# A planner that counts a load as a transfer plus a latency, shorter scale chains, and a new table of ranks

## The chip, the cores and the metric

The kernel runs on one core of a Trainium2 chip. Its engines work side by side: TensorE (PE in the rows) multiplies matrices, VectorE (DVE) and ScalarE (ACT) work elementwise, GpSimd (POOL) does some elementwise work too, and SyncE (SP) issues the DMAs that bring inputs from the device's memory. Each engine takes its own instructions strictly in the order in which they were written, and waits at an instruction until what it needs is there. The metric is the device time of one execution in microseconds (us); three runs and one profiled execution of the kernel before are at hand.

## The reference

Attention with four batches, eight heads, 576 positions and 64 values per head; half the heads see a local band of 32, the other half positions with the same remainder modulo 32. Its output, 2304 tokens of 512 values, goes through two feed-forward blocks.

```python
scores = scale * np.matmul(q, k.transpose(0, 1, 3, 2))
scores = np.where(masks[None, :, :, :], scores, -1000000000.0)
attn = softmax(scores)                       # with a small guard in the sum
x = (attn @ v) as 2304 x 512
h = x @ w_in;   x = np.maximum(0.01 * h, h) @ w_out                       # first block, 2048 wide
h = x @ w_in2;  out = (np.maximum(h, 0.0) + np.log1p(np.exp(-np.abs(h)))) @ w_out2
```

The weights arrive as 64-bit floats, two 32-bit words each.

## The kernel before, in words

**Products.** A float32 product is made of three float16 products: each operand is cut into a high part and the rest (`mm3`, L538 to L541). So a step of a projection is twelve matmuls of 288 columns (four slices of the sum by three), and nearly all of TensorE's time goes into these. Tokens of the first block are worked in eight units of 288 (units 0 and 1 belong to batch 0, 2 and 3 to batch 1, and so on), those of the second in nine of 256.

**Weights.** A quarter of a weight (2 MB) is loaded into one of four areas, `pair` in the rows (`Weight.load`, L156). VectorE finds its largest value (`largest`, L165), TensorE spreads it over the partitions (`to_all`, L131, written `pm`), VectorE works out a power of two (`scale`, about ten instructions on one number per partition, among them a reciprocal and a product, L196 and L197), and then VectorE and ScalarE turn the 64-bit words into a float16 pair: `low` (L171), `copy_sign` (L209) or `sink` (L219), `merge` (L230), `high` (L238), `rest` (L245, L253). The area is then free for the next load. Of the first block's input weight (W1) each quarter has its own scale; the output weights (O1, O2) have one scale over four quarters, so all four quarters of O2 are first loaded once for their largest value alone (`plan_largest`, `O2l`): load, `largest`, load, `largest`, one after another through one area.

**Attention.** For each batch, six pieces: `dots` (L362) on TensorE, the largest of each row on VectorE (`top`, L382, L390), the exponential on ScalarE, sums, a division spread on GpSimd (L464), a transposition on TensorE (`turn`, L473), a copy on ScalarE (`fetch`, L484), the product with v (`pv`, L496), and a cut in high and rest (L524, L531, L535). `factor` works out the batch's scale (L136 to L318).

**What sets the order.** All this is not run by a schedule on the chip: `Plan` is told every step with its engine, a cost in us, what it depends on and a rank name, and `Plan.run` plays the whole through in time, beginning at each engine with the step of lowest rank among those that could start about now. In that order the instructions are written. While TensorE has nothing in this play before 130 us, filler products of 512 columns are written (`idle`, L100). `RANKS` holds for each name a start and a slope. A step on SP is a load: its cost is how long SP's place in the play is taken, and whatever depends on it is counted ready `LOAD` later. The names: `W1r`, `W1m`, `O1r`, `O1m`, `W2`, `O2`, `O2l` are weight steps, `A0` to `A3` and `B0` to `B3` the early and late steps of attention, `G0` to `G3` the first projections of units 0 to 3, `S0` to `S3` the second ones, `M` both of the later units, `X`, `F`, `Fa`, `Fp`, `Fd`, `S`, `E` the second block.

Of the kernel before, what the change touches and what calls it, by code (L numbers as in the profile page):

```python
# [12 lines left out]
I32 = mybir.dt.int32  # L13
# [10 lines left out]
KC = DM // P  # L24
# [10 lines left out]
TINY = 2.0 ** -120  # L35
# [20 lines left out]
SIGNED = ("i1",)  # L56
# [6 lines left out]
def build(tc, qt, kl, ks, v, wi1, wo1, wi2, wo2, mloc, mstr, out):  # L63
    nc = tc.nc
    with ExitStack() as ctx:
# [84 lines left out]
        class Weight:  # L150
# [24 lines left out]
            def scale(self, q, g):  # L175
# [60 lines left out]
            def high(self, q, hl, by=None):  # L236
                by = (1.0 if self.name in SIGNED else SHARE) if by is None else by
                nc.scalar.activation(flat(hl[0]), self.f[q], AF.Copy, scale=by)  # L238
                self.hl[q] = hl

            def rest(self, q):
                hi, lo = self.hl[q]
                if self.name in SIGNED:
# [19 lines left out]
        class Attn:  # L263
# [47 lines left out]
            def factor(self):  # L311
# [3 lines left out]
                inv(self.ax, self.p2, 2.0 ** 14)  # L315
# [25 lines left out]
            def dots(self, half):  # L341
# [3 lines left out]
                ps = two_banks("ps", "sc" if self.b else "mm")  # L345
# [197 lines left out]
        def project(ps, wi, x, f):  # L543
            q, o = divmod(f, 4)
            sl = slice(o * P, (o + 1) * P)
            for c in range(KC):
                mm3(ps, wi.hl[q][0][:, c, sl], wi.hl[q][1][:, c, sl], x[0][:, c, :], x[1][:, c, :], c == 0, c == KC - 1)

        def gate1(x, f, g):
# [4 lines left out]
            def part(i):  # L554
                project(ps[:, i], W1, x, f + i)
# [24 lines left out]
        class Plan:  # L580


            HOP, SLACK, LOAD = 0.2, 0.5, 0.9
# [123 lines left out]
        def plan_loads(A, buf, where, after={}):  # L707
# [3 lines left out]
            for k, n in enumerate((0, 1, "v", 2, 3)):  # L711
                if n == "v":
                    ld[n] = plan.add("SP", 4.05, lambda: A.load_v(buf()), after.get("v", ()), (f"L{b}", k))
# [3 lines left out]
                    "SP", 1.65, lambda n=n, places=places: A.load_qk(n, *(w and w() for w in places)),  # L717
# [7 lines left out]
        def plan_attention(A, ld, after=(), behind=(), scaled=()):  # L725
# [17 lines left out]
            for half in range(6):  # L743
# [4 lines left out]
                    "PE", 2 * n * w / 975 + 0.12 * n * (A.mode[half] != "e"), A.dots, mine + [dots] * (half > 0), half,  # L748
                    take=["sc" if b else "mm"], free=mine * (half % 3 == 2), behind=behind,
# [49 lines left out]
        def plan_together(W, name, after, parts, then, w1):  # L799
# [6 lines left out]
            for q in range(4):  # L806
                ld = plan.add("SP", 5.9, lambda q=q: W.load(q, area(q)), after[q], ("L" + name, q))
# [29 lines left out]
        def plan_quarter(W, name, q, place, after, parts, after_read, then=None):  # L837
# [17 lines left out]
            ld = plan.add("SP", 5.9, lambda: W.load(q, area(place)), after, ("L" + name, q))  # L855
            x = step("DVE", 2.2, big, [ld], 0)
            y = step("PE", 0.1, over, [x], 0, take=["pt"])
            sc = step("DVE", 1.45 if then else 1.05, scale, [y], 0.3, free=[y])
            y = step("DVE", 1.14, lambda: W.low(q), [ld], 0.1, port=True)
            if W.name in SIGNED:  # L860
# [7 lines left out]
            if W.name in SIGNED and REST[q] == "Pool":  # L868
# [3 lines left out]
        def plan_largest(W, name, busy):  # L872
# [3 lines left out]
            for q in range(4):  # L876
                ld = plan.add("SP", 5.9, lambda q=q: W.load(q, area(1)), busy[1], ("L" + name, q))
# [22 lines left out]
        def plan_first(u, after, w, place, rank):  # L900
            b, half = divmod(u, 2)
            out = []
            for f in range(0, NF, 2):
                st = {}

                def products(i, f=f, st=st):
                    if f + i == 0:
                        gs[u] = place()
                    if i == 0:
                        st["then"] = gate1(xpart(at[b], half), f, gs[u])  # L910
                    st["then"][0](i)
# [5 lines left out]
                mm = step("PE", 1.473, lambda p=products: p(0), after + [w[f // 4]], take=["mm"])  # L917
                more = step("PE", 1.473, lambda p=products: p(1), [mm])
                bend = step("ACT", 0.65, then(1), [more], take=["t"], free=[mm])
                high = step("ACT", 0.58, then(2), [bend])  # L920
                rest = step("Pool", 1.25, then(3), [high], free=[bend])
                out += [(mm, high, rest), (more, high, rest)]
# [210 lines left out]
        for q in range(4):  # L1133
            step = lambda eng, cost, fn, deps, k, **kw: plan.add(eng, cost, fn, deps, ("O2", q + k), port=eng == "DVE")
            ld = plan.add("SP", 5.9, lambda q=q: O2.load(q, area(1)), busy[1], ("LO2", 4 + q))
# [319 lines left out]
```

## Time and profile before

| | us |
|---|---|
| median of three runs | 848.12 (845.75 to 849.96) |
| the profiled execution | 852.07 |
| its span, first to last instruction | 850.3 |
| TensorE busy | 827.4 (97% of the span) |
| ScalarE busy | 524.7 (62%) |
| VectorE busy | 488.1 (57%) |
| GpSimd busy | 255.6 (30%) |
| mean granted TensorE clock | 0.994 of full |

TensorE's busy time holds the filler products too, so a busy TensorE early on is not always a working one. The page cuts the span in 40 slices of 21 us: TensorE is at nine tenths or more in all but the first, the thirteenth (250 to 276 us, which shows 7) and the last; VectorE is at eight or nine tenths only up to about 105 us.

```
PE   8999999999997999999999999999999999999997
DVE  5998949634434525764003668776665756465453
DMA  9833320303455204420002200000000000000000
```

### The profile page before, as it was taken

What the parts mean: (1) busy time and instruction counts of PE and PEld (TensorE: products, weight loads), DVE (VectorE), ACT (ScalarE), POOL (GpSimd) and SP (SyncE); (2) the same over time, 40 slices, a digit from 0 to 9 for tenths busy, and PEclk for the clock granted to TensorE, in tenths of its full rate; (3) what the DMA queues carried; (4) which work ended last, traced back from release to release, by engine and by line L of the source; (5) the groups of instructions that cost most, each with busy time, mean ns of one, the idle gap of its engine ahead of it and who ended that gap; (6) DMA issues with size and microseconds to landing.
All of it is one profiled execution on the core that took longest, in us unless ns stands there. A gap on an engine that the chain in (4) does not pass through costs nothing.

```text
span 850.3 us, 17550 instructions
## 1 busy us (share of the span) xinstructions
PE 827.4 (97%) x7311; PEld 680.9 (80%) x7311; DVE 488.1 (57%) x1160; ACT 524.7 (62%) x961; POOL 255.6 (30%) x193
## 2 busy tenths in 40 slices
PE   8999999999997999999999999999999999999997
PEld 4567777777776777777777788888888888888886
DVE  5998949634434525764003668776665756465453
ACT  2799687457754334423416288878676777677671
POOL 2267776123342032001305032232313222222220
PEclk9999999999998999999999999999999999999999
DMA  9833320303455204420002200000000000000000
GB/s 367 371 128 122 136 99 2 133 4 114 153 202 198 100 1 141 158 86 15 2 1 100 99 2 2 25 2 26 2 25 2 25 2 27 1 26 25 3 26 25
DMA packets 10991, 63.27 MB, mean 74 GB/s; under 512 B 1344, under 2 KB 1440, under 8 KB 7840
## 3 DMA queue, kind: packets, MB, share of 16 engines
q1 hardware_dynamic: 10656, 62.00, 19.5%
q8 instruction: 57, 0.93, 0.5%
q14 instruction: 22, 0.18, 0.1%
q10 hardware_dynamic: 256, 0.16, 0.1%
HBM read 57.44 MB, written 4.72 MB: 73 GB/s over the span
## 4 chain that ended last, share of the span: by engine, by line
PE 80%; DVE 9%; DMA 7%; ACT 2%; issue 1%; SPq 1%; POOL 0%; DVEq 0%; ACTq 0%
PE h L539 13%; PE h L541 12%; PE h L540 12%; PE o L541 12%; PE o L539 12%; PE o L540 12%; DMA pair<-wo_dram 4%; PE ps L362 2%; DVE m L165 2%; PE po L496 2%; PE pt L473 1%; DVE s L390 1%; DVE pair L230 1%; DMA pair<-wi_dram 1%; DVE pair L219 1%
## 5 line engine op out<-in xcount | busy, mean ns | idle before, releaser
L539 PE MATMUL h<-x,w 128*128 128x256 f16 (+1 forms) x1088 | 303.7, 279 | 1.7 <-ACT t L560 1.7
L541 PE MATMUL h<-x,w 128*128 128x256 f16 (+1 forms) x1088 | 303.7, 279 | 0.0
L540 PE MATMUL h<-x,w 128*128 128x256 f16 (+1 forms) x1088 | 303.6, 279 | 0.0
L1255 POOL TENSOR_TENSOR pair<-pair,t 128x512 f32<-128x512 f32 x72 | 96.2, 1338 | 268.8 <-ACT t L1251 116.2
L566 POOL TENSOR_TENSOR g<-t,g 128x576 f16<-128x576 f32 x64 | 96.5, 1513 | 214.8 <-ACT g L563 214.8
L539 PE MATMUL o<-g,pair 128*128 128x288 f16 x512 | 147.6, 288 | 0.0
L541 PE MATMUL o<-g,pair 128*128 128x288 f16 x512 | 147.5, 288 | 0.1
L540 PE MATMUL o<-g,pair 128*128 128x288 f16 x512 | 147.5, 288 | 0.0
L1271 DVE SCALAR_TENSOR_TENSOR gr<-pair,x2b,gr 128x896 f16<-128x896 f32 x72 | 85.7, 1195 | 72.6 <-ACT gr L1267 71.4
L540 PEld LDWEIGHTS <-w 128*128 128x128 f16 x1088 | 106.3, 98 | 20.8 <-issue 2.1
L539 PEld LDWEIGHTS <-w 128*128 128x128 f16 x1088 | 106.3, 98 | 19.7
L541 PEld LDWEIGHTS <-w 128*128 128x128 f16 x1088 | 106.3, 98 | 19.7 <-POOL w L245 0.3
L1263 DVE TENSOR_TENSOR pair<-pair 128x128 f32<-128x128 f32 x288 | 75.6, 305 | 45.9 <-POOL pair L1255 43.3
L1267 ACT ACTIVATE gr<-pair,x2b 128x896 f16<-128x896 f32 x72 | 74.2, 1035 | 37.3 <-DVE pair L1263 28.5
L560 ACT ACTIVATE t<-h,gs 128x576 f32<-128x576 f32 x64 | 47.1, 736 | 55.2 <-PE h L541 50.4
L464 POOL TENSOR_TENSOR s<-s,sm 96x512 f32<-96x512 f32 (+3 forms) x48 | 50.5, 1070 | 93.0 <-DVE sm L459 50.0
L1238 ACT ACTIVATE t<-h,x2s 128x512 f32<-128x512 f32 x72 | 49.0, 680 | 43.1 <-PE h L541 42.9
L539 PE MATMUL o<-w,gr 128*128 128x256 f16 x270 | 73.6, 273 | 0.0
L540 PE MATMUL o<-w,gr 128*128 128x256 f16 x270 | 73.6, 273 | 0.0
L541 PE MATMUL o<-w,gr 128*128 128x256 f16 x270 | 73.6, 273 | 0.0
L541 PEld LDWEIGHTS <-pair 128*128 128x128 f16 x512 | 50.3, 98 | 13.4 <-DVE pair L253 0.4
L539 PEld LDWEIGHTS <-pair 128*128 128x128 f16 x512 | 50.4, 98 | 13.1
(136 smaller groups left out, 1350.3 us busy)
## 6 DMA issues: line engine op xcount, KB each, us to landing
pair<-wo_dram SPq DMA_DIRECT2D x12, 2048.0 KB, 8.0
pair<-wi_dram SPq DMA_DIRECT2D x8, 2048.0 KB, 10.0
out_dram<-pair SPq DMA_DIRECT2D x18, 256.0 KB, 2.1
q<-qt_dram SPq DMA_DIRECT2D x12, 288.0 KB, 4.6
v<-v_dram SPq DMA_DIRECT2D x2, 1408.0 KB, 15.1
pair<-v_dram SPq DMA_DIRECT2D x2, 1408.0 KB, 6.4
k<-ks_dram SPq DMA_DIRECT2D x7, 288.0 KB, 6.2
k<-kl_dram SPq DMA_DIRECT2D x5, 304.0 KB, 4.4
```

The lines of the kernel that those rows point to most:

```text
L165: nc.vector.tensor_reduce(out=m, in_=hi.bitcast(F32), axis=AX.XY, op=ALU.max, apply_absolute_value=True)
L464: nc.gpsimd.tensor_tensor(out=sv, in0=sv, in1=rs, op=ALU.mult)
L539: nc.tensor.matmul(ps, ah, bh, start=first, stop=False)
L540: nc.tensor.matmul(ps, ah, bl, start=False, stop=False)
L541: nc.tensor.matmul(ps, al, bh, start=False, stop=last)
L560: nc.scalar.activation(t, ps, AF.Prelu, scale=gates[f // 4], alpha=0.01)
L566: nc.gpsimd.tensor_tensor(out=g[:, 1, f : f + 2, :], in0=t, in1=g[:, 0, f : f + 2, :], op=ALU.subtract)
L1238: nc.scalar.activation(t, self.ps[k], AF.Prelu, scale=self.sc[:, k // 2 : k // 2 + 1], alpha=-1.0)
L1255: nc.gpsimd.tensor_tensor(out=r, in0=r, in1=self.a[k], op=ALU.add)
L1263: nc.vector.tensor_tensor(out=r[:, o], in0=r[:, x], in1=r[:, y], op=op)
L1267: nc.scalar.activation(self.a[k][:, 0], self.r[k][:, 1:], AF.Copy, scale=self.ag)
L1271: nc.vector.scalar_tensor_tensor(out=a[:, 1], in0=self.r[k][:, 1:], scalar=self.ag, in1=a[:, 0], op0=ALU.mult, op1=ALU.subtract)
```

## The change

Four things, of which the last follows from the others:

- `LOAD` goes from 0.9 to 2.6, and the costs of the loads on SP go down: a weight quarter from 5.9 to 5.15, v from 4.05 to 3.4, a pair of q and k from 1.65 to 1.5. Some other costs change by up to 0.2.
- A power of two is inverted by one integer instruction on its bits instead of a reciprocal and a product. This is done in `inv` (attention's `factor`, the second block's `factor` and `scales`) and in `Weight.scale` for W1's four quarters. The other weights keep the two instructions.
- `SIGNED` names quarters instead of a weight (all four of W1, as before); `EARLY` is empty, so the code that asks for it does what it did. `TINY` goes from 2^-120 to 2^-100.
- All numbers of `RANKS` are new (39 names).

```diff
-TINY = 2.0 ** -120
+TINY = 2.0 ** -100
...
-    "O1r": (-2072.090, 3.859), ... "W2": (870.356, 188.158), "X": (881.188, 1.772),
+    "O1r": (-3595.719, 0.065), ... "W2": (-3968.496, 59.142), "X": (854.645, 2.549),
...
-SIGNED = ("i1",)
+SIGNED = (("i1", 0), ("i1", 1), ("i1", 2), ("i1", 3))
+EARLY = ()
...
-        def inv(a, p2, mul):
-            nc.vector.reciprocal(out=a, in_=p2)
-            nc.vector.tensor_scalar(out=a, in0=a, scalar1=mul, scalar2=None, op0=ALU.mult)
+        def inv(a, p2, power):
+
+            nc.vector.tensor_scalar(
+                out=a.bitcast(I32), in0=p2.bitcast(I32), scalar1=-1.0, scalar2=(254.0 + power) * 2 ** 23,
+                op0=ALU.mult, op1=ALU.add,
+            )
...
-                nc.vector.reciprocal(out=s, in_=t)
-                nc.vector.tensor_scalar(
-                    out=s, in0=s, scalar1=2.0 ** -110 if self.name in SIGNED else 2.0 ** -98 / SINK, scalar2=None, op0=ALU.mult
-                )
+                if (self.name, q) in SIGNED:
+                    inv(s, t, -110)
+                else:
+                    nc.vector.reciprocal(out=s, in_=t)
+                    nc.vector.tensor_scalar(out=s, in0=s, scalar1=2.0 ** -98 / SINK, scalar2=None, op0=ALU.mult)
...
-            HOP, SLACK, LOAD = 0.2, 0.5, 0.9
+            HOP, SLACK, LOAD = 0.2, 0.5, 2.6
...
-                clock = collections.defaultdict(float, SP=1.7, PE=5.7)
+                clock = collections.defaultdict(float, SP=1.4, PE=5.7)
...
-                ld = plan.add("SP", 5.9, lambda q=q: W.load(q, area(1)), busy[1], ("L" + name, q))
+                ld = plan.add("SP", 5.15, lambda q=q: W.load(q, area(1)), busy[1], ("L" + name, q))
```

The order moves on every engine; the numbers of products, loads and attention steps stay. Filler products number 84 instead of 72, all of them still ahead of the first projection. Three places follow; the changed file's lines lie a few further down.

**GpSimd, batch 3's attention.** L464 (L469) spreads a piece of batch 3, L566 (L571) is the rest of a first projection, one for every two steps of TensorE. Before:

```order
L464 TENSOR_TENSOR s<-s,sm 96x512 x6
L464 TENSOR_TENSOR s<-s,sm 126x504
L566 TENSOR_TENSOR g<-t,g 128x576
L464 TENSOR_TENSOR s<-s,sm 126x504
L566 TENSOR_TENSOR g<-t,g 128x576 x7
L464 TENSOR_TENSOR s<-s,sm 108x432 x2
L464 TENSOR_TENSOR s<-s,sm 108x216 x2
L566 TENSOR_TENSOR g<-t,g 128x576 x24
```

Now:

```order
L469 TENSOR_TENSOR s<-s,sm 96x512 x6
L571 TENSOR_TENSOR g<-t,g 128x576 x16
L469 TENSOR_TENSOR s<-s,sm 126x504 x2
L469 TENSOR_TENSOR s<-s,sm 108x432 x2
L469 TENSOR_TENSOR s<-s,sm 108x216 x2
L571 TENSOR_TENSOR g<-t,g 128x576 x16
```

Between batch 3's third and fourth piece stand the first projections of two units (32 steps of TensorE) where that of one stood (16 steps).

**VectorE, the loads of O2 for its largest value.** L165 (L169) is `largest`, m_2947 (m_3211) the four values of O2, L531 (L536) the rest of a piece of batch 3, L1184 (L1198) a step of the second block. Before (a first `largest` of the four stands 17 rows higher, ahead of batch 3's tops):

```order
L1184 TENSOR_REDUCE m<-x_2137 128x1
L454 TENSOR_SCALAR sm<-sm,ix_2273,gx_2274 126x8
L459 RECIPROCAL sm<-sm 126x8
L165 TENSOR_REDUCE m_2947<-pair_128 128x1 x3
L935 TENSOR_SCALAR xs<-p2x_843,k_o_1711 128x1
L531 SCALAR_TENSOR_TENSOR x<-po,ax_2266,x 128x2x192
L390 ISA s,mx<-ps,ms 108x108
```

Now:

```order
L464 RECIPROCAL sm<-sm 96x8
L1198 TENSOR_REDUCE m<-x_2085 128x1
L169 TENSOR_REDUCE m_3211<-pair_128 128x1 x4
L889 TENSOR_REDUCE m<-m_3211 128x1
L169 TENSOR_REDUCE m<-pair_128 128x1
L949 TENSOR_SCALAR xs<-p2x_594,k_o_1659 128x1
L175 TENSOR_SCALAR pair_128<-pair_128 128x2048
L137 TENSOR_REDUCE g<-pm 128x1
```

The four `largest` of O2 stood around batch 3's tops and rests; now they stand together, with W2's first quarter (the second L169) behind them, ahead of every step of batch 3's fourth piece. On TensorE the `pm` that the last row waits for stands 32 first-projection steps, one `dots`, one `pv`, one `turn` and one second-projection step after batch 2's last `pv`, three second-projection steps and two turns.

**VectorE, up to the end of batch 0's attention.** L535 (L540) over 18x6 is batch 0's last rest, on which the first projection waits together with W1's first quarter (L245, L250). Before:

```order
L535 TENSOR_TENSOR x<-po,x 128x18x6 x2
L450 TENSOR_SCALAR sm<-sm 96x8
L459 RECIPROCAL sm<-sm 96x8
L171 TENSOR_SCALAR pair_128<-pair_128 128x2048
L209 TENSOR_SCALAR pair_128<-pair_128 128x2048
L450 TENSOR_SCALAR sm<-sm 96x8
```

Now:

```order
L137 TENSOR_REDUCE g<-pm 128x1
L141 TENSOR_SCALAR g<-g 128x1
L124 TENSOR_SCALAR p2x_594<-g 128x1
L146 TENSOR_SCALAR ax_595<-p2x_594 128x1
L322 TENSOR_SCALAR ix_601<-p2x_594 128x1
L323 TENSOR_SCALAR gx_602<-ix_601 128x1
L175 TENSOR_SCALAR pair_128<-pair_128 128x2048
L455 TENSOR_SCALAR sm<-sm 96x8
L464 RECIPROCAL sm<-sm 96x8
L214 TENSOR_SCALAR pair_128<-pair_128 128x2048
L395 ISA s,mx<-ps,ml 96x128
```

`low` and `copy_sign` of W1's second quarter (L171 and L209, now L175 and L214), batch 1's `factor` (L137 to L323) and the guard of batch 1's first piece stood behind batch 0's last rest; now they stand ahead of it, by one group of tops and the rest itself. `factor` has one instruction (L146) where L144 and L145 stood.

## Rows read from the trace of the kernel before

**Rows 1.** Busy time by stretch: engine busy us (instructions), TensorE clock, DMA share, GB/s

```profile
50.00:60.00 10.00, 9.61 (x83) 7.57 (x83) 9.93 (x8) 8.55 (x15) 8.18 (x4) 1.00 0.50 206
60.00:70.00 10.00, 7.75 (x83) 6.01 (x81) 9.83 (x44) 9.50 (x30) 8.76 (x5) 1.00 0.27 84
80.00:90.00 10.00, 8.68 (x81) 6.66 (x78) 7.70 (x29) 8.33 (x24) 10.00 (x7) 1.00 0.64 206
90.00:100.00 10.00, 9.60 (x95) 7.34 (x94) 9.31 (x17) 7.08 (x22) 7.42 (x7) 1.00 0.32 129
140.00:150.00 10.00, 9.23 (x77) 7.11 (x76) 10.00 (x4) 8.39 (x9) 4.88 (x3) 1.00 0.01 3
270.00:280.00 10.00, 9.36 (x67) 6.94 (x64) 4.16 (x32) 5.07 (x22) 1.77 (x2) 0.66 0.58 210
```

**Rows 2.** What TensorE waited for: us in total, times, longest us

```profile
PE po L496 <- DVE x L531: 3.9, 1, 3.9
PE ps L362 <- DVE mx L390: 2.2, 3, 1.2
PE ps L362 <- DMA k<-ks_dram: 1.7, 3, 0.7
PE ps L362 <- DMA k<-kl_dram: 0.9, 1, 0.9
```

**Rows 3.** Chain of waits, 220 to 272 us: start us, us, what

```profile
223.75 10.57 DMA pair<-wo_dram
236.67 9.03 DMA pair<-wo_dram
248.04 7.68 DMA pair<-wo_dram
258.06 8.72 DMA pair<-wo_dram
...
269.21 0.52 DVE x L531
```

**Rows 4.** Busy time by stretch, the two us after TensorE's longest wait

```profile
272.00:274.00 2.00, 2.00 (x13) 1.48 (x11) 0.74 (x3) 2.00 (x8) 0.00 (x0) 0.50 0.94 401
```

**Rows 5.** Timeline of TensorE: start us, us, engine, line, what

```profile
49.66 0.30 PE L539 MATMUL h<-x,w 128*128 128x288 f16 x1
...
51.14 0.29 PE L539 MATMUL h<-x,w 128*128 128x288 f16 x1
...
221.61 0.59 PE L496 MATMUL po<-a,pair 108*64 108x108 f32 x8
222.18 1.12 PE L362 MATMUL ps<-k,q 64*96 64x128 f32 x16
...
261.19 0.88 PE L496 MATMUL po<-a,pair 128*64 128x96 f32 x16
```

**Rows 6.** Timeline of VectorE, 48 to 66 us

```profile
48.41 0.44 DVE L535 TENSOR_TENSOR x<-po,x 128x108 f16<-128x108 f32 x2
...
49.08 1.18 DVE L171 TENSOR_SCALAR pair<-pair 128x2048 uint32<-128x2048 uint32 x1
50.29 3.23 DVE L209 TENSOR_SCALAR pair<-pair 128x2048 uint16<-128x2048 uint16 x1
...
63.94 0.28 DVE L136 TENSOR_REDUCE g<-pm 128x1 f32<-128x128 f32 x1
...
64.63 0.17 DVE L144 RECIPROCAL ax<-p2x 128x1 f32<-128x1 f32 x1
64.83 0.15 DVE L145 TENSOR_SCALAR ax<-ax 128x1 f32<-128x1 f32 x1
...
65.15 2.28 DVE L165 TENSOR_REDUCE m<-pair 128x1 f32<-128x2048 f32 x1
```

**Rows 7.** Timeline of VectorE, the chain of O1's first quarter

```profile
129.12 0.29 DVE L136 TENSOR_REDUCE g<-pm 128x1 f32<-128x128 f32 x1 [1.01 <-PE pm L131]
...
145.16 3.37 DVE L253 SCALAR_TENSOR_TENSOR pair<-pair,by_o 128x2048 f16<-128x2048 f32 x1
```

More of the change, by code (lines that the diff above doesn't have):

```diff
@@ L552, in gate1, with part @@
             t = None
-            def part(i):
-                project(ps[:, i], W1, x, f + i)
+            def part(i, cs=range(KC)):
+                project(ps[:, i], W1, x, f + i, cs)
             def bend():
@@ L747, in plan_attention @@
                 dots = step(
-                    "PE", 2 * n * w / 975 + 0.12 * n * (A.mode[half] != "e"), A.dots, mine + [dots] * (half > 0), half,
-                    take=["sc" if b else "mm"], free=mine * (half % 3 == 2), behind=behind,
+                    "PE", (2 * n * w / 975 if half < 3 else 0.2 + 2 * n * w / 1150) + 0.12 * n * (A.mode[half] != "e"), A.dots, mine + [dots] * (half > 0), half,
+                    take=["sc" if b or EARLY and half > 2 else "mm"], free=mine * (half % 3 == 2), behind=behind,
                 )
@@ L806, in plan_together @@
             for q in range(4):
-                ld = plan.add("SP", 5.9, lambda q=q: W.load(q, area(q)), after[q], ("L" + name, q))
+                ld = plan.add("SP", 5.15, lambda q=q: W.load(q, area(q)), after[q], ("L" + name, q))
                 big = step("DVE", 2.2, lambda q=q: W.largest(q, m()[:, q : q + 1]), [ld], q)
@@ L853, in scale @@
                     then(q)
-            ld = plan.add("SP", 5.9, lambda: W.load(q, area(place)), after, ("L" + name, q))
+            ld = plan.add("SP", 5.15, lambda: W.load(q, area(place)), after, ("L" + name, q))
             x = step("DVE", 2.2, big, [ld], 0)
             y = step("PE", 0.1, over, [x], 0, take=["pt"])
-            sc = step("DVE", 1.45 if then else 1.05, scale, [y], 0.3, free=[y])
+            sc = step("DVE", (1.35 if then else 1.1) - 0.15 * ((W.name, q) in SIGNED), scale, [y], 0.3, free=[y])
             y = step("DVE", 1.14, lambda: W.low(q), [ld], 0.1, port=True)
-            if W.name in SIGNED:
+            if (W.name, q) in SIGNED:
                 y = step("DVE", 2.35, lambda: W.copy_sign(q), [y], 0.2, port=True)
@@ L916, in plan_first @@
                 step = lambda eng, cost, fn, deps, **kw: plan.add(eng, cost, fn, deps, rank(f), **kw)
-                mm = step("PE", 1.473, lambda p=products: p(0), after + [w[f // 4]], take=["mm"])
-                more = step("PE", 1.473, lambda p=products: p(1), [mm])
-                bend = step("ACT", 0.65, then(1), [more], take=["t"], free=[mm])
+                if f in early:
+                    local = [after[3], after[7], after[8]]
+                    mm = step(
+                        "PE", 1.473, lambda p=products: [p(i, (0, 1)) for i in range(2)], local + [w[f // 4]], take=["mm"]
+                    )
+                    more = step("PE", 1.473, lambda p=products: [p(i, (2, 3)) for i in range(2)], after + [mm])
+                    first = more
+                else:
+                    mm = first = step("PE", 1.473, lambda p=products: p(0), after + [w[f // 4]], take=["mm"])
+                    more = step("PE", 1.473, lambda p=products: p(1), [mm])
+                bend = step("ACT", 0.76, then(1), [more], take=["t"], free=[mm])
                 high = step("ACT", 0.58, then(2), [bend])
                 rest = step("Pool", 1.25, then(3), [high], free=[bend])
-                out += [(mm, high, rest), (more, high, rest)]
+                out += [(first, high, rest), (more, high, rest)]
             return out
@@ L1134, in build @@
             step = lambda eng, cost, fn, deps, k, **kw: plan.add(eng, cost, fn, deps, ("O2", q + k), port=eng == "DVE")
[L1135 removed]
+            ld = plan.add("SP", 5.15, lambda q=q: O2.load(q, area(1)), busy[1], ("LO2", 4 + q))
             y = step("DVE", 1.14, lambda q=q: O2.low(q), [ld], 0.1)
@@ L1330, in build @@
             rank = lambda n, k: (n, u * NK + k)
-            y = plan.add("DVE", 1.3, U.largest, moved(u), rank("X", 0), behind=highs[-2:-1])
+            y = plan.add("DVE", 1.15, U.largest, moved(u), rank("X", 0), behind=highs[-2:-1])
             over = plan.add("PE", 0.1, U.over, [y], rank("X", 0), take=["mm"])
-            y = plan.add("DVE", 0.75, U.factor, [over], rank("X", 0), free=[over])
+            y = plan.add("DVE", 0.82, U.factor, [over], rank("X", 0), free=[over])
             xh = plan.add("ACT", 1.15, U.high, [y] + products(7) * (u == 0), rank("X", 0), take=["x2"], behind=highs[-1:])
```

39 lines of the change are left out of this document (20 added, 19 removed), and 20 rows, old and new, of the table RANKS.

## Prediction

> **What bounds the kernel now.** I read the page's busy shares first: TensorE is busy 97% of the span, so the end is set by TensorE's work plus whatever time it loses, and a new order can only move the loss. The table of stretches [rows 1] and TensorE's waits [rows 2] show where that is. Between 50 and 100 us it is idle 0.39 + 2.25 + 1.32 + 0.40 = 4.36 us [rows 1], with VectorE busy 9.8 of 10 us in the worst of these stretches: the front is VectorE's. At 140 to 150 us it is idle 0.77 us [rows 1]. Later it waits for q and k, 1.7 + 0.9 = 2.6 us [rows 2]. The largest single wait, 3.9 us, is for a VectorE instruction of batch 3's attention, L531 [rows 2]. The chain of waits [rows 3] shows what that instruction was late for: it stood in VectorE's queue behind the `largest` of O2's quarters, each of which stood still until its 2 MB load landed, 10.57, 9.03, 7.68 and 8.72 us after issue. It is a wait for DMA under VectorE's name. It cost more than its length: TensorE's granted clock, full everywhere else shown, is 0.50 of 2.4 GHz, the 1.2 GHz level, two us behind it [rows 4] and 0.66 on average over 270 to 280 us, so 0.34 x 10 = 3.4 us of work were lost there, beside 0.64 us idle [rows 1]. This one place cost 3.9 + 3.4 + 0.64 = 7.9 us.
>
> **The change part by part.** A twelve-matmul step takes 51.14 - 49.66 = 1.48 us [rows 5].
>
> *The loads of O2.* Now 32 first-projection steps, which need nothing new of VectorE, stand where VectorE stands still for the loads, and with W2's first `largest` there are five loads in a row. Time both from the end of batch 3's third `dots`, 222.18 + 1.12 = 223.30 [rows 5]. The chain: the first load landed at 223.75 + 10.57 = 234.32, 11.0 later [rows 3]; it has the same q and k loads beside it now. From landing to the next issue is 236.67 - 234.32 = 2.35. The three later loads took (9.03 + 7.68 + 8.72) / 3 = 8.48 on average. With four more of them W2's maximum stands at 11.0 + 2.35 + 4 x (8.48 + 2.35) = 56.7. TensorE's cover up to the `pm` that needs it: 36 steps x 1.48 = 53.3, a `dots` of 1.12, two `pv` of 0.59 and 0.88 [rows 5], three turns estimated at 0.5 each from the short groups beside them: 57.4. So the wait is gone by a hair; I put 0.2 for it. Bounds: with four loads at 7.68 the chain is 53.5, no wait; at 9.03 it is 58.9, a wait of 1.5; at 10.57 it is 65.0, a wait of 7.6. The gain is 7.9 - 0.2 = 7.7. What is late next is batch 3's fourth tops behind W2's steps; TensorE has 7 us of second-projection steps there to cover them.
>
> A sentence of the Trainium skill on this, "DMA: Bandwidth & Descriptors", "Anatomy of one DMA": a load costs a fixed 2.0 us plus its bytes at 436 GB/s, which for 2 MB would be 6.8 us (an estimate of that page). By it the chain would be 50.0 and no wait could come back. The trace does not agree: the shortest of these loads took 7.68 [rows 3], and the measurement decides.
>
> *The front.* Ahead of batch 0's last rest, on which the first projection waits, VectorE now has W1's second `low` and `copy_sign` (1.2 and 3.0, from start to start; 3.23 busy), `factor` of batch 1 (65.15 - 63.94 = 1.21) [rows 6] and a guard (0.3). Off come 0.2 for each pair of scale instructions that became one (64.63 to 64.83 is a slot) [rows 6], twice in W1's scales and once in `factor`. So 5.7 - 0.6 = 5.1 more. VectorE's small idle stretches ahead of it, some 0.5, should fill: the first projection starts 4.6 after 49.66 [rows 5]. TensorE has 1.7 us of batch 1's turns and `pv` in that time which stood later: net 2.9 lost. In return, those steps are out of the way of batch 1's tops, for which TensorE waited longest in the front (1.2 of the 2.2 in rows 2). Going through TensorE's new order by hand with VectorE's durations as they were, I find 0.8 for the fifth `dots` (two steps on O1's first quarter stand ahead of its tops), 0.5 for a turn, 0.4 for a PSUM bank, 0.2 for batch 1's last rest: 1.9 in place of 4.36. So 2.9 - 2.5 = 0.4 lost. Bounds: 2.9 lost if nothing is recovered, 1.5 gained if the front's waits go entirely.
>
> *O1's first quarter.* From VectorE's first instruction after `pm` to the end of the first rest is 145.16 + 3.37 - 129.12 = 19.4 us [rows 7], in the same order as before. Twelve steps cover it, 17.8; three turns that stood there are gone. So a wait of 1.6 in place of 0.77 [rows 1]: 0.8 lost; bounds 0 and 2.
>
> The Trainium skill's "SBUF — State Buffer", "SBUF: two separate sides", says that GpSimd and a VectorE instruction in certain modes hold a shared port exclusively, so that the other fully waits. In this trace the chain's rest took 3.37 [rows 7], which would be such a wait; how many it meets in the new order no row shows. By the page this term would lie at the upper end, 2.
>
> *q and k.* These waits follow two loads issued when the `dots` before free their buffers. In the new order turns and a `pv` are added to the three steps behind them for batch 2, some 1.9 us, and about 0.3 for batch 3. Of 2.6 I leave 1.0: 1.6 gained, bounds 0 and 2.6.
>
> *The scale chains.* 26 pairs become single instructions (four W1 scales, four `factor`, nine units with two). 0.2 us each is 5 us of VectorE. Behind 100 us VectorE is idle four tenths of the time and TensorE has products queued, so I cost that at nothing; if that cover were gone, a unit of the second block would gain 0.4. The new instruction is not in the trace; it is bounded by 0.15 of L145 [rows 6] and by the pair's 0.35, so it can't lose.
>
> *The rest.* In the second block the first projection runs as far ahead of the second for the first unit's steps as before or less (by my count of steps 10 us against 15 for the third), where the longest wait of the pair in the profile came with 8 us. I count nothing. The tail keeps its order.
>
> Sum: -7.7 + 0.4 + 0.8 - 1.6 = -8.1. The sum is against the profiled execution, 852.07, which is 3.95 above the median of the runs, 848.12. Taken off the median that gives 840.0; as an absolute time, if the 3.95 were lost at the very place that goes, 844.0. The row of the loads shows that they vary by 3 us from one to the next, so some of the extra may well be theirs. I take the middle, 842.0, and lean to 842.3 for waits I have not seen.
>
> **The rivals.**
>
> *The loads are late again.* Loads of 9.03 on average make TensorE wait 1.5 at W2's `pm`; with the steps on batch 3's tops that follow behind, 2.2. If the clock falls as it did after 3.9 [rows 4], another 3.4: 5.6 given back, 847.9. For it: three of four loads took longer than 8.7 [rows 3], and the plan's 7.75 is near the shortest. Against it: two of the four had q and k beside them, and waits of 1.2 and 0.9 [rows 2] left the clock full.
>
> *The front gives nothing back.* VectorE stays the bound up to 100 us, and what it does first only moves the wait: 2.9 lost instead of 0.4, O1's wait at 2. Then 842.3 + 2.5 + 1.2 = 846.0. For it: VectorE's 9.8 of 10 [rows 1]. Against it: the same steps are all due before 100 us in both orders.
>
> *Slower: five loads in a row block VectorE.* All of W2's first quarter and batch 3's fourth piece now stand behind O2's loads. If loads run like the slowest, 10.57, TensorE waits 7.6 at the `pm`, loses the clock for 3.4 and then waits for tops, about 1: 842.3 - 0.2 + 12.0 = 854.1. It decides from a mean of 9.9 per load, where the wait passes 5 us and the gain is used up with the clock's fall. For it: there are five, each behind the one before, so a slow stretch adds up. Against it: the 10.57 was the only one with q and k loads issued around it.
>
> **How the numbers follow.** 0.5% of 848 is 4.2 us, about what a measurement of this kernel can tell. The forecast has 0.53, with a range of its own from 838.5 to 846; the late loads 0.17; the front 0.14; the slower case 0.12; 0.04 is left for what I have not seen. Faster by over 0.5%, below 843.9: most of the forecast's share, 0.48, and 0.04 of others, 0.52. Within: 0.05 of the forecast and most of the first two rivals, 0.33. Slower, above 852.3: 0.15. The range goes from 838.5, the forecast's lower end, to 850, which takes in the first two rivals and leaves out the slower case.
>
> **What would show it.** Right: no wait of TensorE for L536 (the old L531) above 1 us; the granted clock full from 200 to 400 us; the wait for `pm` of W2's first quarter below 1.5 us, with VectorE's `largest` waiting for five loads in a row; the first projection near 54 us with under 2.5 us idle between it and 100 us; a wait of 1 to 2 us at the first second-projection step. Wrong: a wait of several us at W2's `pm` or at the `dots` behind it with a clock of 0.5, or a first projection near 54 us and over 4 us idle behind it. It would also be wrong if new waits stood in the second block, for which I count nothing.

## The result, and the profile after

The changed kernel takes 839.1 us, the median of four runs (838.91 to 839.46), where the kernel before took 847.04 in the four runs beside them (845.75 to 849.96): a ratio of 0.9902, with a 95% interval from 0.9873 to 0.9931. The forecast was 842.3 with a range from 838.5 to 850. So the change makes the kernel faster, by 7.9 us, and the time is 3.2 us below the forecast. As a gain that is 7.9 where 848.12 - 842.3 = 5.8 was forecast: the kernel before, too, is 1.1 us faster in these four runs than in the three that the forecast started from. A later pair on another chip gave 839.34 (838.91 to 840.0, six runs) against 846.53 (844.23 to 849.25, eleven runs), 0.9911 (0.9891 to 0.9931).

The profiled execution took 838.91 us, 0.2 from its median; that of before took 852.07. In the two profiles the difference is therefore 13.2 us, and 5 of it belong to the run of before that happened to be profiled. Where that comes from is shown by the profiles of the first two experiments.

First the page of the changed kernel: its span, the engines' busy time with their shares and instructions, and TensorE with its granted clock in 40 slices of 21 us.

```profile
span 837.1 us, 17534 instructions
...
PE 825.3 (99%) x7323; PEld 681.8 (81%) x7323; DVE 486.1 (58%) x1134; ACT 523.3 (63%) x961; POOL 256.0 (31%) x193
...
PE   9999999999999999999999999999999999999997
...
PEclk9999999999999999999999999999999999999999
```

The 7 in the thirteenth slice of before is gone, and so is every slice at a lower clock. TensorE idles 837.1 - 825.3 = 11.8 us where it idled 850.3 - 827.4 = 22.9.

To see from which part of the program this comes, the span is cut into the same six stretches in both kernels; the columns are the length, TensorE's busy us (instructions), its clock, the DMA share and GB/s. Before:

```profile
0.00:100.00 100.00, 91.82 (x803) 1.00 0.62 239
100.00:150.00 50.00, 49.23 (x420) 1.00 0.12 44
150.00:250.00 100.00, 97.42 (x913) 1.00 0.32 110
250.00:300.00 50.00, 45.46 (x392) 0.93 0.43 164
300.00:700.00 400.00, 398.99 (x3469) 1.00 0.10 38
700.00:860.00 160.00, 144.50 (x1324) 0.99 0.05 18
```

After:

```profile
0.00:100.00 100.00, 95.06 (x828) 1.00 0.55 218
100.00:150.00 50.00, 49.21 (x403) 1.00 0.25 88
150.00:250.00 100.00, 99.83 (x926) 1.00 0.16 57
250.00:300.00 50.00, 50.00 (x413) 1.00 0.61 226
300.00:700.00 400.00, 399.84 (x3562) 1.00 0.12 45
700.00:860.00 160.00, 131.35 (x1204) 0.99 0.04 14
```

Of the first 100 us one thing must be taken off: busy time there holds the filler products. Here are the rows of the fillers alone, the first of before and the second of after:

```profile
0.00:100.00 100.00, 19.62 (x72) 1.00 0.62 239
```

```profile
0.00:100.00 100.00, 22.82 (x84) 1.00 0.55 218
```

Read with that, stretch by stretch, idle time before less idle time after:

| stretch, us | worked out | gained, us |
|---|---|---|
| 0 to 100, the front | 8.18 - 4.94, less 22.82 - 19.62 of fillers | 0.0 |
| 100 to 150, O1's first quarter | 0.77 - 0.79 | 0.0 |
| 150 to 250, q and k | 2.58 - 0.17 | 2.4 |
| 250 to 300, O2's loads | 4.54 - 0, and 0.07 x 50 of the clock | 8.0 |
| 300 to 700, the second block | 1.01 - 0.16 | 0.9 |
| 700 on, the tail | 5.8 - 5.75 | 0.1 |
| sum | | 11.4 of 13.2 |

The other 1.8 us is busy time, and most of it is waiting too. In a step a matmul starts 0.12 us behind the one ahead of it but is recorded as 0.29 us long, so the first 0.16 us of a stop behind it count as busy. Here is such a stop after the change:

```profile
142.09 0.29 PE L545 MATMUL o<-g,pair 128*128 128x288 f16 x1
143.17 0.30 PE L546 MATMUL o<-g,pair 128*128 128x288 f16 x1 [0.79 <-DVE pair L258]
```

From start to start this is 1.08 us, 0.96 more than in a step, of which 0.79 is shown as idle. Behind matmuls of the projections the starts show 11 stops before and 3 after: 8 x 0.16 = 1.3 of the 1.8.

Now the rows that answer to single steps. TensorE's waits after the change (us in total, times, longest), to be laid beside [rows 2]:

```profile
PE h L544 <- ACT t L565: 0.9, 1, 0.9
PE o L546 <- DVE pair L258: 0.8, 1, 0.8
PE ps L367 <- DVE mx L395: 0.4, 2, 0.2
```

The wait for batch 3's rest (L531, now L536) is gone, and so is every wait for a DMA. The tops (L390, now L395) are down from 2.2 to 0.4. The turns' wait for ScalarE's copy, which [rows 2] does not list, is down from the row here to 1.7 in 5 waits:

```profile
PE pt L473 <- ACT a L484: 2.9, 7, 0.7
```

The first projection's first matmul, and the stretches that answer to [rows 1], all engines (PE, PEld, DVE, ACT, POOL busy us, TensorE's clock, DMA share, GB/s):

```profile
54.84 0.30 PE L544 MATMUL h<-x,w 128*128 128x288 f16 x1
```

```profile
50.00:60.00 10.00, 9.47 (x97) 6.84 (x94) 9.97 (x36) 9.87 (x34) 3.33 (x4) 1.00 0.69 244
...
70.00:80.00 10.00, 9.09 (x82) 7.12 (x82) 9.65 (x29) 8.53 (x31) 8.51 (x6) 1.00 0.77 279
...
270.00:280.00 10.00, 10.00 (x84) 7.98 (x83) 1.40 (x2) 4.27 (x6) 5.01 (x4) 1.00 0.59 211
```

VectorE's timeline at O2's loads (start, us, engine, line, what, and in brackets how long it stood idle and for what), answering to [rows 3]:

```profile
258.87 2.29 DVE L169 TENSOR_REDUCE m<-pair 128x1 f32<-128x2048 f32 x1 [2.66 <-DMA pair<-wo_dram]
...
268.83 2.29 DVE L169 TENSOR_REDUCE m<-pair 128x1 f32<-128x2048 f32 x1 [7.68 <-DMA pair<-wo_dram]
...
279.73 2.29 DVE L169 TENSOR_REDUCE m<-pair 128x1 f32<-128x2048 f32 x1 [8.61 <-DMA pair<-wo_dram]
...
289.79 2.29 DVE L169 TENSOR_REDUCE m<-pair 128x1 f32<-128x2048 f32 x1 [7.77 <-DMA pair<-wo_dram]
...
299.70 2.29 DVE L169 TENSOR_REDUCE m<-pair 128x1 f32<-128x2048 f32 x1 [7.44 <-DMA pair<-wi_dram]
```

VectorE still stands still for the loads, 2.66 + 7.68 + 8.61 + 7.77 + 7.44 = 34.2 us of it. That now costs nothing, because TensorE has first projections to do meanwhile. TensorE's timeline at the two ends of this cover:

```profile
246.75 1.12 PE L367 MATMUL ps<-k,q 64*96 64x128 f32 x16 [0.17 <-DVE mx L395]
...
304.35 0.22 PE L132 MATMUL pm<-idb,m 128*128 128x128 bf16 x1
```

From the end of batch 3's last `dots` ahead of the loads, 247.87, W2's maximum stood at 299.70 + 2.29 = 301.99, 54.1 later. TensorE came to the `pm` that needs it at 304.35, 56.5 later, and did not wait. The margin is 2.4 us, about a third of one load; in the profiles of e9 and e6, two more runs of this order, it is 2.3 and 1.9.

Last, VectorE's timeline from the first instruction to the last of the chain of O1's first quarter, answering to [rows 7]:

```profile
124.53 0.29 DVE L137 TENSOR_REDUCE g<-pm 128x1 f32<-128x128 f32 x1 [1.98 <-PE pm L132]
...
126.31 1.05 DVE L1036 TENSOR_SCALAR by_o<-by_o,r 128x4 f32<-128x4 f32 x1
...
139.74 3.37 DVE L258 SCALAR_TENSOR_TENSOR pair<-pair,by_o 128x2048 f16<-128x2048 f32 x1
```

It takes 139.74 + 3.37 - 124.53 = 18.6 us where it took 19.4. All of the 0.8 between lies in one instruction on four numbers per partition, which took 1.88 us before and 1.05 now (in e10, in the old order, 1.22):

```profile
130.90 1.88 DVE L1022 TENSOR_SCALAR by_o<-by_o,r 128x4 f32<-128x4 f32 x1
```

### The profile page after: what moved, and what is told of

The parts are those of the page before. It is cut to its first block, busy times and chain, and to the rows that moved or that the text cites. A ratio compares the mean times of both kernels' runs of the same rounds, so it can differ in the third digit from the quotient of the medians.

```text
span 837.1 us, 17534 instructions
## 1 busy us (share of the span) xinstructions
PE 825.3 (99%) x7323; PEld 681.8 (81%) x7323; DVE 486.1 (58%) x1134; ACT 523.3 (63%) x961; POOL 256.0 (31%) x193
## 4 chain that ended last, share of the span: by engine, by line
PE 85%; ACT 5%; DMA 5%; DVE 4%; issue 0%; SPq 0%; POOL 0%; DVEq 0%; ACTq 0%
PE o L544 13%; PE o L546 13%; PE o L545 13%; PE h L544 13%; PE h L546 13%; PE h L545 13%; DMA v<-v_dram 3%; PE po L501 2%; PE ps L367 2%; PE pt L478 1%; DMA pair<-wi_dram 1%; ACT s L447 1%; ACT gr L1281 1%; DVE pair L224 1%; DVE pair L1317 1%; DVE pair L235 1%
## 5 line engine op out<-in xcount | busy, mean ns | idle before, releaser
L1269 POOL TENSOR_TENSOR pair<-pair,t 128x512 f32<-128x512 f32 x72 | 93.9, 1304 | 270.7 <-ACT t L1265 123.2
L571 POOL TENSOR_TENSOR g<-t,g 128x576 f16<-128x576 f32 x64 | 99.9, 1567 | 202.4 <-ACT g L568 202.4
L1277 DVE TENSOR_TENSOR pair<-pair 128x128 f32<-128x128 f32 x288 | 71.7, 290 | 36.1 <-POOL pair L1269 33.6
L1281 ACT ACTIVATE gr<-pair,x2b 128x896 f16<-128x896 f32 x72 | 74.4, 1035 | 17.8 <-DVE pair L1277 15.2
L469 POOL TENSOR_TENSOR s<-s,sm 96x512 f32<-96x512 f32 (+3 forms) x48 | 47.8, 1016 | 89.9 <-DVE sm L464 40.6
L169 DVE TENSOR_REDUCE m<-pair 128x1 f32<-128x2048 f32 x16 | 36.4, 2276 | 52.7 <-DMA pair<-wo_dram 37.6
L546 PEld LDWEIGHTS <-pair 128*128 128x128 f16 x512 | 50.1, 98 | 13.8 <-DVE pair L258 1.1
```

The lines of the kernel that those rows point to most:

```text
L169: nc.vector.tensor_reduce(out=m, in_=hi.bitcast(F32), axis=AX.XY, op=ALU.max, apply_absolute_value=True)
L469: nc.gpsimd.tensor_tensor(out=sv, in0=sv, in1=rs, op=ALU.mult)
L546: nc.tensor.matmul(ps, al, bh, start=False, stop=last)
L571: nc.gpsimd.tensor_tensor(out=g[:, 1, f : f + 2, :], in0=t, in1=g[:, 0, f : f + 2, :], op=ALU.subtract)
L1269: nc.gpsimd.tensor_tensor(out=r, in0=r, in1=self.a[k], op=ALU.add)
L1277: nc.vector.tensor_tensor(out=r[:, o], in0=r[:, x], in1=r[:, y], op=op)
```

## Experiments

Line numbers differ by a few from kernel to kernel; the names of the tiles stay.

**The scale chains alone (e1).** The kernel before with the one-instruction inversion and the new `TINY`, and nothing else. Costs and ranks are those of before, so the order is the same but for 26 instructions fewer on VectorE.

```diff
...
-        def inv(a, p2, mul):
-            nc.vector.reciprocal(out=a, in_=p2)
-            nc.vector.tensor_scalar(out=a, in0=a, scalar1=mul, scalar2=None, op0=ALU.mult)
+        def inv(a, p2, power):
+
+            nc.vector.tensor_scalar(
+                out=a.bitcast(I32), in0=p2.bitcast(I32), scalar1=-1.0, scalar2=(254.0 + power) * 2 ** 23,
+                op0=ALU.mult, op1=ALU.add,
+            )
...
```

> The kernel before with the one-instruction inversions alone; ranks, costs and every other instruction stay in place. Theory (the gain is O2's loads under cover): 847.0 within 1.5, the wait for L531 and the clock of 0.5 behind it still there. Rival (the shorter chains are the gain): 840 to 844.

Measured: 845.08 (842.49 to 848.57, ten runs) against 846.48 of before (843.45 to 849.21, nineteen runs), ratio 0.9985 (0.9964 to 1.0006). No difference that can be told from none, though the interval would leave room for 3 us. Its profile is worth more than its time, since it shows the old order in a run with other load times. First TensorE's wait, then two stretches of 10 us, as above:

```profile
PE po L500 <- DVE x L535: 1.6, 1, 1.6
```

```profile
260.00:270.00 10.00, 7.78 (x68) 5.89 (x66) 6.19 (x27) 5.71 (x22) 1.31 (x2) 0.86 0.53 198
270.00:280.00 10.00, 10.00 (x98) 7.90 (x97) 5.28 (x14) 3.68 (x13) 3.59 (x4) 0.97 0.10 43
```

The wait for batch 3's rest is 1.6 us where it was 3.9 in [rows 2], and the clock lost (0.14 + 0.03) x 10 = 1.7 us where it lost 3.4: O2's loads took 9.48, 7.63, 7.60 and 8.00 us here, against the four of [rows 3]. With the 2.22 us idle from 260 to 270 us this place cost 3.9 us, not 7.9. So what this place costs the old order changes from run to run with the loads, and the profiled run of before had an expensive one. With q and k it is the same: from 150 to 250 us TensorE idles 1.17 us here and 2.58 in the profile of before. These two places make 5.4 of the 5.9 us by which the two spans differ (844.4 and 850.3).

**O2's first loads alone (e2, and again as e10).** The kernel before with one number changed, the planner's cost of the four loads for the largest value. All ranks, `LOAD` and the two-instruction chains stay.

```diff
-                ld = plan.add("SP", 5.9, lambda q=q: W.load(q, area(1)), busy[1], ("L" + name, q))
+                ld = plan.add("SP", 9.0, lambda q=q: W.load(q, area(1)), busy[1], ("L" + name, q))
```

> The kernel before with one number changed: the four loads of O2 for its largest value cost 9.0 in the plan instead of 5.9, so with LOAD of 0.9 they are counted 9.9 long. The order up to batch 3's fourth dots is the old one; behind it, batch 3's second and third rests stand ahead of the fourth largest. Theory: the wait of 3.9 for L531 and the clock's fall go, 7.9 us off a profile like the one of before, so 840 to 844; the waits for q and k and the front stay as they were. Rival (the front is the gain): 847 within 1.5, and any wait saved here comes back at another step of batch 3.

> The kernel before with one number changed, the cost of O2's first loads (5.9 to 9.0), beside the changed kernel on one chip. Theory (O2's loads are a little over half of the change): 841.5 to 843, which is 4 to 5 below the kernel before and 2 to 4 above the changed one. Rival (the loads are all of it): within 1 us of the changed kernel.

> The changed kernel as it is, beside the kernel before with only the cost of O2's first loads raised to 9.0, on one chip, to measure what the change brings beyond those loads. Theory (the rest of the new order, q and k and the second block above all, brings 3 us): 838.9 to 839.7, and 2 to 4 us below the other kernel of this pair. Rival (the loads are all of it, and the 3 us between runs on different chips are a difference of chips): within 1 us of the other kernel.

Measured: e2 842.08 (841.23 to 844.79, ten runs), ratio 0.9954 (0.9938 to 0.9971). In the pair on one chip, e10 took 842.63 (841.26 to 843.63), the changed kernel (e9) 839.34 (838.91 to 840.0), the kernel before 846.53. The two do not overlap. So O2's loads are 846.53 - 842.63 = 3.9 of the 7.2 us, and the rest of the change is 3.3: the theory, against the rival that the loads are all of it. TensorE's own instructions stand in e2 and e10 in the order of before, but for two first-projection steps, which now stand ahead of a `dots` of batch 3, and one `pm`. In e2's profile the place is clean:

```profile
260.00:280.00 20.00, 20.00 (x201) 15.95 (x199) 8.92 (x41) 11.21 (x40) 4.11 (x5) 1.00 0.40 151
```

What the rest of the change still has to win is seen in e10, in one of TensorE's waits and in two stretches, the third and the fifth of the six above:

```profile
PE o L541 <- DVE gr L1271: 0.8, 1, 0.8
```

```profile
150.00:250.00 100.00, 98.48 (x925) 1.00 0.36 125
...
300.00:700.00 400.00, 398.45 (x3474) 1.00 0.10 38
```

It still idles 1.52 us where q and k are loaded and 1.55 in the second block; the changed kernel idles 0.17 and 0.16 there. But these are waits of one run: e2, the same kernel, idles 0.81 and 0.43 there. So here are all the kept profiles of the old order (before, e1, e2, e10) beside those of the new one (after, e9, and e6 and e5 further down). In the table the front is the idle time up to 100 us with the fillers added, the next three rows are idle time alone, and the last is TensorE's busy time without the fillers, from the profiles in which the clock stayed full:

| us | old order | new order | gained, of means |
|---|---|---|---|
| 0 to 100, the front | 27.80, 27.70, 28.09, 27.83 | 27.76, 28.84, 28.24, 27.94 | -0.3 |
| 100 to 150 | 0.77, 0.12, 0.15, 0.13 | 0.79, 0.79, 0.80, 0.80 | -0.5 |
| 150 to 250, q and k | 2.58, 1.17, 0.81, 1.52 | 0.17 in all four | 1.35 |
| 300 to 700, the second block | 1.01, 1.19, 0.43, 1.55 | 0.16 in three; in e5 its own wait stands here | 0.9 |
| busy without fillers | 804.19, 804.37 (e2, e10) | 802.46, 802.48, 802.50 (after, e9, e6) | 1.8 |
| sum | | | 3.2 |

That comes near the 3.3 of the pair. The busy time is again mostly short loss that no idle row shows. By the starts of TensorE's matmuls, of the 1.9 between e10 and e9 some 1.0 is in 9 stops in place of 3, each with 0.16 counted as busy. Some 0.6 is in 23 changes in place of 17 from a step to a product of attention, which cost about 0.1 each (in e10 one starts at 101.06 behind a matmul of 100.85, 0.21 later and not 0.12). These are sums over stretches: no run isolates one of them.

**One load more (e5).** The changed kernel, with the last of the four loads done twice into the same area. The planner is told nothing of it, so the order is the same, and the chain of loads grows by one.

```diff
-                ld = plan.add("SP", 5.15, lambda q=q: W.load(q, area(1)), busy[1], ("L" + name, q))
+                ld = plan.add("SP", 5.15, lambda q=q: [W.load(q, area(1)) for _ in range(1 + (q == 3))],
+                              busy[1], ("L" + name, q))
```

> The changed kernel with the fourth of O2's quarters loaded twice into its area, the second load behind the first; the plan doesn't know of it and the order on the other engines is unchanged. In the changed kernel's trace W2's maximum was there 54.1 us after batch 3's third dots, TensorE came to it 56.5 after. Theory (O2's loads are hidden with 2.4 us to spare): the load adds 8, so TensorE waits 5.6 at pm, and its clock falls as in the kernel before, some 3 more: 846 to 849. Rival (the cover is wider than it looks, or batch 3's steps behind can be taken up): 839 to 841.

Measured: 847.16 (845.75 to 848.21, ten runs), ratio to before 1.0007 (0.9986 to 1.0028). That is 8.1 above the changed kernel's 839.1, and 7.6 above e6, which ran on the same chip in the changed kernel's order: one load gives all of the gain back. The wait, the two stretches behind it, and VectorE's timeline at the last two loads:

```profile
PE pm L132 <- DVE m L169: 5.4, 1, 5.4
```

```profile
300.00:310.00 10.00, 4.95 (x58) 3.77 (x56) 2.59 (x3) 2.38 (x4) 2.30 (x2) 0.97 0.56 210
310.00:320.00 10.00, 9.67 (x75) 7.20 (x77) 8.59 (x33) 5.53 (x19) 0.00 (x0) 0.68 0.01 2
```

```profile
298.14 2.29 DVE L169 TENSOR_REDUCE m<-pair 128x1 f32<-128x2048 f32 x1 [15.89 <-DMA pair<-wo_dram]
...
307.99 2.29 DVE L169 TENSOR_REDUCE m<-pair 128x1 f32<-128x2048 f32 x1 [7.37 <-DMA pair<-wi_dram]
```

The doubled load lets VectorE stand 15.89 us where it stood 7.77, 8.1 longer. Less the margin of 2.4 that leaves 5.7 of TensorE; it waited 5.4, and the 0.16 that counts as busy. The clock then cost (0.03 + 0.32) x 10 = 3.5. This is the slower rival's mechanism, at its place and nearly at its price. It shows that the cover is real and that it is short.

**The chains in the new order (e6).** The changed kernel with the reciprocal and the product again (and the old `TINY`), everything else as changed.

```diff
...
-                inv(self.ax, self.p2, 14)
+                inv(self.ax, self.p2, 2.0 ** 14)
...
-                inv(self.ag, self.pb, 13)
+                inv(self.ag, self.pb, 2.0 ** 13)
...
-                    inv(s, t, -110)
+                    inv(s, t, 2.0 ** -110)
```

> The changed kernel with reciprocal and product in place of the one-instruction inversion, all else and the order the same. Theory (the chains are hidden): 839.1 to 840.0; in the front up to 0.6 can show. Rival (the chains are the gain): 843 or more.

Measured: 839.61 (838.77 to 839.97, six runs), ratio to before 0.9925 (0.9899 to 0.9951). VectorE is busy 490.4 us with 1160 instructions where it was 486.1 with 1134. This lies 0.3 to 0.5 us above the changed kernel's two medians, which are from other chips, with ranges that overlap: no difference that can be told from none. TensorE's waits in its profile are those of the changed kernel within 0.1 us, so 4.3 us of VectorE stay hidden.

**New ranks for the front, old ranks for the rest (e3).** The changed kernel with the numbers of before for all names but A0, A1, B0, B1, W1m, W1r, O1m, O1r, L0, L1, LW1, LO1, G0 to G3 and S0. It was meant to isolate the front.

```diff
-    "O2": (852.091, 2.607), "O2l": (49.180, 200.000),
+    "O2": (-2880.992, 200.000), "O2l": (-1535.625, 0.177),
...
```

> The changed kernel with the old ranks for all names but the front's (A0, A1, B0, B1, W1, O1, G0 to G3, S0 and their loads); the order is the new one up to about 95 us, and batch 3 has one unit's 16 steps in it again. Theory: the front is even (within 1.5 of before) and the loss is in the middle, so this stays at 843 to 848, with the L531 wait smaller than before since the plan's loads are 7.75 and no longer 6.8. Rival (the front is the gain): 839 to 841.

Measured: 913.54 (913.23 to 914.35, four runs), ratio 1.0793 (1.0765 to 1.0822). Both expectations missed by far. Most of the loss is neither in the front nor at O2's first loads: from 300 to 700 us TensorE is idle for 56.6 us. TensorE's longest waits, and a stretch:

```profile
PE h L573 <- ACT pair L1286: 18.8, 5, 14.2
PE o L573 <- ACT pair L1169: 16.6, 2, 11.6
```

```profile
480.00:500.00 20.00, 8.01 (x72) 6.84 (x70) 7.78 (x20) 5.56 (x4) 0.00 (x0) 0.82 0.00 0
```

Here L1169 is O2's conversion (L1140 of the changed kernel) and L1286 the second block's own work on ScalarE. The old numbers for these steps, played through with the new costs, seem to put the second block's start and O2 in each other's way, a place that neither kernel had trouble with.

**Old ranks for the front, new ranks for the rest (e4).** The mirror image.

```diff
-    "A0": (-3335.562, 49.059), ... "G0": (-3079.071, 12.095),
+    "A0": (-3169.380, 0.030), ... "G0": (-2647.248, 31.363),
```

> The changed kernel with the old ranks for the front's names and the new ones for the rest: the 32 first-projection steps stand over O2's loads as in the changed kernel. Theory: no wait for L536 (the old L531), clock full, 838 to 842. Rival (the front is the gain): 845 or more with full clock in the middle, the loss all ahead of 110 us.

Measured: 862.95 (862.79 to 865.24, four runs), ratio 1.02 (1.0171 to 1.023). The theory missed. In form this is the rival's result, the loss ahead of some 110 us and the clock full in the middle, but the front that loses is not the old one. A stretch of it:

```profile
40.00:60.00 20.00, 13.02 (x91) 8.33 (x91) 18.29 (x57) 15.11 (x35) 1.12 (x3) 0.74 0.30 110
```

The old numbers with the new costs do not give the old front: the plan writes 68 fillers, not 72, and TensorE idles 7.0 us at 40 to 60 and 5.9 at 80 to 100 us, where the kernel before idles 0.7 and 1.7. The middle was in order, with no wait for batch 3's rest. So this run says nothing of the front's share.

**All costs without the ranks (e7), all ranks without the costs (e8).** One execution each. e7 is the changed kernel with the whole old table; e8 is the kernel before with the short chains and the whole new table.

```diff
 # e7, against the changed kernel
-    "O2": (852.091, 2.607), "O2l": (49.180, 200.000),
+    "O2": (-2880.992, 200.000), "O2l": (-1535.625, 0.177),
...
 # e8, against the kernel before (with e1's edit beside it)
-    "O2": (-2880.992, 200.000), "O2l": (-1535.625, 0.177),
+    "O2": (852.091, 2.607), "O2l": (49.180, 200.000),
...
```

> The changed kernel with all the old ranks: new costs, new LOAD, one-instruction chains. Its front has the order of the run with the old front, with 68 fillers. Theory (a table of ranks is good only for the costs it was searched with): 855 to 870, the loss ahead of 120 us, no wait for L536 in batch 3. Rival (the right latency helps by itself): 840 to 845.

> The kernel before with the one-instruction chains and all the new ranks: old costs, old LOAD. The plan writes 108 fillers in place of 84, among them some behind the first projection. Theory (ranks and costs belong together): 850 to 870. Rival (the ranks carry the gain alone): 838 to 842.

Measured: e7 940.4, which is worse than expected by some 70 us: it has the losses of e3 and of e4 together (from 500 to 640 us TensorE is busy 83.53 of 140 us, at a clock of 0.79). e8 took 866.41, as expected. Its two largest waits and the stretch of the second:

```profile
PE h L543 <- ACT t L564: 6.8, 3, 3.4
PE pm L131 <- DVE m L168: 4.4, 1, 4.4
```

```profile
300.00:320.00 20.00, 15.60 (x110) 11.44 (x108) 8.08 (x13) 6.18 (x9) 6.39 (x5) 0.84 0.30 112
```

The `pm` wait is W2's first quarter behind O2's loads, the place of the slower rival: with loads counted at 5.9 and 0.9 the same ranks write a cover that is too short by 4.4 us.

## Why the prediction was right, and by how much it was off

**O2's loads: right.** The step said that a wait under VectorE's name was a wait for four loads, that 32 first projections would cover it, and that five loads in a row would just fit. The chain was put at 56.7 us and the cover at 57.4; they measured 54.1 and 56.5. The loads between cost (299.70 - 258.87) / 4 = 10.2 from one to the next, where 8.48 + 2.35 = 10.8 was taken. The 0.2 that was left for a wait did not come. e2 shows that this place alone gives 3.9 to 4.4 us in medians. The 7.9 of this term was read correctly from the profiled run, but that run is an expensive one. The prediction saw this and took half of the 3.95 off; e1's profile has 3.9 at the same place, so the full 3.95 could have come off this term. The cost by which the prediction comes to 6.8 us per load is given by the Trainium skill ("DMA: Bandwidth & Descriptors", "Anatomy of one DMA") for DMAs that GpSimd issues. These loads are SyncE's, and none took under 7.4 us (e5).

**The front: near nothing, as said.** The first projection started at 54.84 us; 54.3 was forecast. Between 50 and 100 us 1.44 us are idle (two of the five stretches have any), where 1.9 was forecast and 4.36 was before. The term was +0.4; the balance shows 0.0 between the two profiles, a loss of 1.0 between those of e10 and e9, and 0.3 between the means of four profiles each.

**O1's first quarter: the wait over-sized, and set beside the wrong one.** A wait of 1.6 was forecast; it was 0.8. The cover of twelve steps, 17.8, was right; the chain was put at the 19.4 of [rows 7], and took 18.6 with a last `rest` as slow as then, 3.37. The 0.8 between is the single instruction shown above; why it took longer before, no run tells. The 0.77 of [rows 1] that the prediction took for O1's wait was for the most part another, a turn that waits for ScalarE:

```profile
144.79 0.52 PE L473 MATMUL pt<-ident,s 96*128 96x96 f32 x4 [0.67 <-ACT a L484]
```

In e1, e2 and e10, in the same order, this stretch idles 0.12 to 0.15. So nothing was lost against the profile of before, and 0.5 against the mean of four. That this is near the 0.8 of the term is luck: the wait was half as long as forecast, and most of what it was set beside was not O1's.

**q and k: right that the waits go, under-sized against the profile.** 1.0 was left for them; none is left. Over the whole stretch 2.4 us went between the two profiles, where the term was 1.6. Against the mean of the four old profiles it is 1.35: the 2.6 of [rows 2] belonged to that run.

**The second block: the step that failed.** "I count nothing", said the prediction. It idles 0.9 us less from 300 to 700 us, between the two profiles and between the means. A short wait there, 0.8 us for L1271, stands in the profiles of before, e1 and e10 and not in the changed kernel's, nor in e2's.

**The chains: right.** Neither e1 nor e6 shows a difference: 0.9985 with an interval that holds 1, and 839.61 in the changed kernel's range.

Together, against the profile's 852.07, the sum was -8.1 and the profiles differ by 13.2: 0.3 of the missing 5.1 is O2's wait and clock, 0.4 the front, 0.8 O1, 0.8 q and k, 0.9 the second block, and 1.8 the busy time that no stretch shows. That last term was not in the forecast at all: it added up idle time, and a stop of TensorE is longer than its idle time and a change of product costs about 0.1 us without any. In medians the forecast was 3.2 too high, 1.1 of it because the kernel before was taken at 848.12 and not at 847.04. Against the profile, all these misses lie on the gaining side; beside the means of the old order the front, O1 and q and k come near their terms, and what is missing is the second block and the busy time, 2.7 together.

**The rivals.** Late loads and the slower case did not come: VectorE stood 7.4 to 8.6 us for each of the last four loads. e5 and e8 show both to be real: a chain 8.1 us longer costs 8.1, and a cover too short by 4.4 costs its wait and the clock. The front's rival, 2.9 lost, is not borne out. On q and k beside the loads the prediction contradicts itself: by the trace of before only the 10.57 had such loads issued around it, and the 9.03 had none beside it.

**What stays open.** The 3.3 us beside O2's loads are placed by adding up profiles, not by experiments. e3 and e4 were to split them and could not, since half a table of ranks gives another plan altogether.

## What to carry to other kernels

When an engine that takes its work in order is named as the releaser of a wait, look at what it was doing ahead of that instruction: here it stood still for a load, and once the planner counted such a load longer (9.9 us in e2, 7.75 with new ranks in the changed kernel) independent products stood beside it. The tables of ranks and costs belong together here: with either one, or half the ranks, exchanged, the kernel was 2 to 11% slower than before. One cost alone can still be put right, as e2 shows. Read more than one profile before sizing a wait: under one order q and k's stretch idled from 0.81 to 2.58 us. And time a hidden chain against its cover as well as against nothing: the last of these loads was hidden with 1.9 to 2.4 us to spare, less than a third of a load.

## What the runs showed of the hardware

O2's first loads, 2 MB each from SyncE's queue, took from 7.4 us (e5) to 10.6 (before) from issue to landing. In [rows 3], in e1 and after the change the first of the four, issued right behind loads of q and k, was the longest (10.57, 9.48, 9.57); but one without any beside it took 9.03 in [rows 3] and 9.56 in e9. Between before and e1 this moved one place of one order by 4 us. On one chip the kernel before spread over 5.0 us (844.23 to 849.25), e10 over 2.4 and the changed kernel over 1.1. That fits with what TensorE still waits for, O2's loads and those of q and k, those of q and k alone, and none; no run shows it to be the cause.

TensorE's granted clock fell behind a wait of only 1.6 us with another of 0.64 close by (e1, 0.86 over 260 to 270 us, so part of it at the 1.2 GHz level), behind 3.9 us in the kernel before (0.50 two us behind it, the 1.2 GHz level) and behind 5.4 us in e5 (0.68 over the next 10 us). It stayed full behind single waits of 0.8 and 0.9 us in the changed kernel and of 1.2 us in e2. In e1 and e5 the loss by the clock, 1.7 and 3.5 us, was as large as the wait itself or two thirds of it.
